# Another order of the partitions between a 64-point and a 47-point DFT, in a kernel of a Fourier layer and an MLP

## The chip, the cores and the metric

The kernel runs on one core of one Trainium2 chip, as one program with one launch. The metric is the device time of one execution in microseconds; a time given for a kernel is the median of several runs. Beside the times there is one profiled execution, from which the spans, the busy times and the waits come.

## The reference

The input is `x`, 8 batches of 3008 tokens with 256 features, in float32. A Fourier layer works along the tokens, and a two-layer MLP follows on every token:

```
X  = rfft(x, axis=1)
Yr = Xr @ w_r - Xi @ w_i + b_r
Yi = Xr @ w_i + Xi @ w_r + b_i
Y  = soft threshold of Yr and of Yi by 0.01
y  = irfft(Y, n=3008, axis=1)
h  = y @ w_in            # 256 -> 2048
out = (h * cos(h)) @ w_out   # 2048 -> 256
```

## The kernel before

**The transform.** 3008 is 64 x 47, and 64 and 47 have no common factor, so the DFT of length 3008 is a DFT-64 and a DFT-47 over a two-dimensional index (n1, n2), with no twiddle factors in between. The host sorts the tokens of `x` by this index (n2 padded from 47 to 48) and, at the end, sorts the output back. Every matmul operand is split into a high and a low part in fp32r; a product is three matmuls, high x high, high x low and low x high.

A batch goes through three stages, and between them through two scratch arrays in device memory, `scr1` and `scr2`:

- **Stage A** (`stage_a`, lines 257 to 295) is the DFT-64. A chunk `c`, of 12, loads 128 partitions x 512 (`xt`, L266; the partitions are two groups g of 64 values n1, the 512 are two values of n2 and 256 features), splits it (`prep`, L268 to 275: a cast to `xh` on VectorE, the residue `xl` on VectorE or GpSimd), multiplies with the constant `f1` (L289 to 291), copies the result out of PSUM to `ao` (L293) and stores it to `scr1` (L294, 256 KB). The output partitions are a real or imaginary part, a group g and a frequency s of 32: 2 x 2 x 32 = 128. In `f1` they are in the order (part, group, s).
- **Stage B** (`stage_b`, lines 298 to 483) is the DFT-47, the complex weights, the threshold and the inverse DFT-47. It loads two frequencies s at a time from `scr1`, as 96 partitions (part, n2) x 2 x 256 (`at`, L306, 192 KB, 16 of a batch), and stores 16 pieces of 192 KB (`bo`, L449) to `scr2`, which is [4 (part, group), 24 (n2), 32 (s), 256].
- **Stage C** (`stage_c`, lines 488 to 531) is the inverse DFT-64. It loads one of the 24 values of n2 at a time from `scr2`, as 128 partitions (part, group, s) x 256 (`bt`, L497, 128 KB; two loads fill one `bt` tile, four make a block of 512 tokens), casts and splits them (`bh`, L503; `bl`), multiplies with the constant `ei` (L521, L522) and leaves `xTh` and `xTl`, 512 tokens with the features on the partitions, for the MLP.

The **MLP** (`moe_step` and `second`, lines 537 to 580) takes the six token blocks of a batch one after the other, with 16 steps of 128 hidden features each.

**The order of the work.** Stages are Python generators that yield an estimated cost after each piece. The prologue runs `stage_a(0)`, then `stage_b(0)` with `stage_a(1)` woven in and with part of the preparation of the MLP's weights (`raw`, L172), then `stage_c(0, 0)`. From there the MLP steps lead: each pulls pieces from `ahead(b)` (lines 615 to 637) as a budget allows. `ahead(b)` yields stage C of the batch's next token blocks, stage B of batch b + 1 and stage A of batch b + 2, and at the end, after a gap, stage C of the first block of batch b + 1. The moment at which the MLP goes from batch b to b + 1 is called a batch turn here; there are seven. Around a turn the loads for two token blocks, eight `bt` loads, follow each other on the queue.

All loads and stores of the stages and the MLP's output stores are issued by SyncE (SP), in one queue; the constants and the tables `f2` are issued by GpSimd. The `TileContext` is built with `schedule_with_timeline_sim=True` (L692): a planner with modelled durations writes the order on each engine. The prologue's tiles come from one pool of five buffers (`XP_BUFS`), which `xt`, `ao`, the Fourier weights and stage B's `at` and `bo` of batch 0 share in turn; later batches use four buffers for loads (`xt`, `at` and `bt` together) and three for results.

How a store or a load walks its two sides is set by these lines:

```
        dst = scr1[b].rearrange("s (r i) d -> r s i d", r=4)                    # L259
            ... dma_start(dst[:, :, 2 * c:2 * c + 2, :], ao ...)                # L294
                nc.sync.dma_start(ld[hf][:, j], scr2[b][:, 4 * t + 2 * hf + j]) # L497
```

The device memory side of the stage A store thus has 4 (part, group) outermost, then 32 s, then a run of 512 numbers; that of the stage C load has 4 outermost, then 32 rows of 256 numbers that follow each other in memory.

Of the kernel before, what the change touches and what calls it, by code (L numbers as in the profile page):

```python
# [19 lines left out]
NB, N, D, FF = 8, 3008, 256, 2048  # L20
# [29 lines left out]
def _split(a):  # L50
    hi = _r11(a)
    return hi, _r11(a - hi.astype(np.float64))
# [7 lines left out]
def _constants():  # L60
    n1, s = np.arange(64), np.arange(32)
    ang = 2 * np.pi * (np.outer(n1, s) % 64) / 64
    f1 = np.zeros((2, 64, 2, 2, 32))
    ei = np.zeros((2, 2, 32, 2, 64))
    alt = (-1.0) ** n1
    for g in range(2):
        f1[g, :, 0, g, :] = np.cos(ang)
        f1[g, :, 1, g, :] = -np.sin(ang)
        f1[g, :, 1, g, 0] = alt
        ei[0, g, :, g, :] = np.cos(ang).T  # L70
        ei[1, g, :, g, :] = -np.sin(ang).T
        ei[1, g, 0, g, :] = alt
    f1 = f1.reshape(128, 128)
    ei = ei.reshape(128, 128) * (2.0 / N)
    crt = {(k % 64, k % 47): k for k in range(N)}
    th = 2 * np.pi * (np.outer(np.arange(47), np.arange(47)) % 47) / 47
    C, S = np.cos(th), np.sin(th)
    f2 = np.zeros((32, 2, 48, 2, 48))
    sig = np.ones((32, 48))
    for sl in range(1, 32):  # L80
        for k2 in range(47):
            sig[sl, k2] = 1 if crt[sl, k2] <= N // 2 else -1
        f2[sl, 0, :47, 0, :47] = C
        f2[sl, 1, :47, 0, :47] = S
        f2[sl, 0, :47, 1, :47] = -S * sig[sl, :47]
        f2[sl, 1, :47, 1, :47] = C * sig[sl, :47]
    i1 = np.zeros((2, 2, 48, 2, 48))
    i1[1, 0, :47, 0, :47] = C
    i1[1, 0, :47, 1, :47] = S
    i1[1, 1, :47, 0, :47] = -S  # L90
    i1[1, 1, :47, 1, :47] = C
    for r, k1 in ((0, 0), (1, 32)):
        for j in range(24):
            c = r * 24 + j
            sig[0, c] = 1 if crt[k1, j] <= N // 2 else -1
            f2[0, r, :47, 0, c] = C[:, j]
            f2[0, r, :47, 1, c] = -S[:, j] * sig[0, c]
            i1[0, 0, c, r, :47] = (0.5 if j == 0 else 1.0) * C[j]
            if j:
                i1[0, 1, c, r, :47] = -S[j]  # L100
    f2 = np.concatenate([f2, f2[:, :, :, :1] + f2[:, :, :, 1:]], 3)
    f2 = f2.reshape(32, 96, 144).transpose(1, 0, 2)
    i1 = i1.reshape(2, 96, 96).transpose(1, 0, 2)
    c_f1 = np.stack(_split(f1), 1)
    c_f3 = np.concatenate(_split(f2), 2)
    c_f2 = np.concatenate(_split(f2[:, :, :96]), 2)
    c_i1 = np.stack(_split(i1), 1)
    c_ei = np.concatenate(_split(ei), 1)
    c_sig = np.concatenate([np.ones((48, 32)), sig.T]).astype(np.float32)
    return [np.ascontiguousarray(a) for a in (c_f1, c_f2, c_i1, c_ei, c_sig, c_f3)]  # L110
# [3 lines left out]
def tile_body(ctx: ExitStack, tc, x, w_r, w_i, b_r, b_i, w_in, w_out,  # L114
              c_f1, c_f2, c_i1, c_ei, c_sig, c_f3, out):
    nc = tc.nc
# [9 lines left out]
    f1 = cp.tile([128, 2, 128], F32R, name="f1")  # L126
# [4 lines left out]
    ei = cp.tile([128, 256], F32R, name="ei")  # L131
# [76 lines left out]
    def rest_pool(lo, x, hi):  # L208
        return nc.gpsimd.tensor_tensor(out=lo, in0=x, in1=hi.bitcast(F32), op=ALU.subtract)  # L209
# [4 lines left out]
    scr1, scr2 = {}, {}  # L214
# [3 lines left out]
    def fps(name):  # L218
        if "pro" in pool:
            if not banks:  # L220
                banks.extend(("f", "h", "o0", "f", "h", "o1", "f", "h"))
            tag = banks.pop(0)
            return ps.tile([128, 512], F32, tag=tag, name=name, bufs=1 if tag[0] == "o" else 3)
        return ps.tile([128, 512], F32, tag="f", name=name, bufs=3)

    def stage_in(name, b=0):
        if b == 0:
            return pool["pro"].tile([128, 512], F32, tag="xp", name=name, bufs=XP_BUFS)
        return wk.tile([128, 512], F32, tag="xt", name=name, bufs=4)

    def stage_out(name, b):
        if b == 0:
            return pool["pro"].tile([128, 512], F32, tag="xp", name=name, bufs=XP_BUFS)
        return wk.tile([128, 512], F32, tag="ao", name=name, bufs=3)
# [19 lines left out]
    mark = {}  # L254


    def stage_a(b):
        scr1[b] = dr.tile([32, 96, 256], F32, tag="scr1", name=f"scr1_{b}")
        dst = scr1[b].rearrange("s (r i) d -> r s i d", r=4)  # L259
        ld = {}  # L260

        def load(c):
            if c < 12:
                ld[c] = stage_in("xt", b)
                with tc.issue_after(mark["at"].ins) if b == 1 and c < 4 else ExitStack():
                    nc.sync.dma_start(ld[c], x[b, :, 512 * c:512 * (c + 1)])  # L266

        def prep(c):  # L268
            if c < 12:
                xt = ld.pop(c)  # L270
                xh = wk.tile([128, 512], F32R, tag="xh", name="xh", bufs=3)
                xl = wk.tile([128, 512], F32R, tag="xl", name="xl", bufs=3)
                nc.vector.tensor_copy(xh, xt)  # L273
                mark[b, c] = (rest if b < 2 and c not in POOL_REST else rest_pool)(xl, xt, xh)
                ld[c] = (xh, xl)

        ahead = XP_BUFS if b == 0 else 1
        for c in range(ahead):
            load(c)
        if b:  # L280
            yield 0.0
        prep(0)
        yield 1.0
        for c in range(12):
            load(c + ahead)
            prep(c + 1)
            xh, xl = ld.pop(c)
            p = fps("pa")
            mm(p, f1[:, 0], xh, start=True, stop=False)  # L289
            mm(p, f1[:, 1], xh, start=False, stop=False)  # L290
            mm(p, f1[:, 0], xl, start=False, stop=True)
            ao = stage_out("ao", b)
            nc.scalar.copy(ao, p)  # L293
            mark[b, "out"] = nc.sync.dma_start(dst[:, :, 2 * c:2 * c + 2, :], ao.rearrange("p (i d) -> p i d", i=2))  # L294
            yield 0.65


# [190 lines left out]
    def stage_c(b, t):  # L488
        th = pool["mo"].tile([128, 2, 512], F32R, tag="xTh", name="xTh", bufs=2)
        tl = pool["mo"].tile([128, 2, 512], F32R, tag="xTl", name="xTl", bufs=2)  # L490
        xT[b, t] = (th, tl)
        ld = {}

        def load(hf):
            ld[hf] = wk.tile([128, 2, 256], F32, tag="xt", name="bt", bufs=4)
            for j in range(2):
                nc.sync.dma_start(ld[hf][:, j], scr2[b][:, 4 * t + 2 * hf + j])  # L497

        def prep(hf):
            bt = ld.pop(hf)  # L500
            bh = wk.tile([128, 2, 256], F32R, tag="xh", name="bh", bufs=3)
            bl = wk.tile([128, 2, 256], F32R, tag="xl", name="bl", bufs=3)
            nc.vector.tensor_copy(bh, bt)  # L503
            rest_pool(bl, bt, bh)
            ld[hf] = (bh, bl)

        load(0)
        load(1)
        yield 2.5
        prep(0)  # L510
        yield 1.0
        for hf in range(2):
            if hf == 0:
                prep(1)
            bh, bl = ld.pop(hf)
            for j in range(2):
                p = fps("pc")
                pv = p.rearrange("p (c h n) -> p c h n", c=2, h=2)
                for c in range(2):
                    cs = slice(128 * c, 128 * c + 128)  # L520
                    mm(p[:, 256 * c:256 * c + 256], bh[:, j, cs], ei, start=c == 0, stop=False, skip_group_check=True)  # L521
                    mm(p[:, 256 * c:256 * c + 128], bl[:, j, cs], ei[:, :128], start=False, stop=c == 1,  # L522
                       skip_group_check=True)
                o = (2 * hf + j) * 128
                hv, lv = pv[:, :, 0], pv[:, :, 1]
                thv, tlv = th[:, :, o:o + 128], tl[:, :, o:o + 128]
                nc.scalar.copy(thv, hv)
                tt = wk.tile([128, 2, 128], F32, tag="tc", name="tc", bufs=2)
                nc.vector.tensor_tensor(out=tt, in0=hv, in1=thv.bitcast(F32), op=ALU.subtract)
                nc.vector.tensor_tensor(out=tlv, in0=lv, in1=tt, op=ALU.add)  # L530
                yield 0.43
# [114 lines left out]
    for b in range(NB):  # L646
        fa = ahead(b)
        for t in range(NTT):
# [20 lines left out]
            while open_[0]:  # L669
                c = next(fa, None)  # L670
# [30 lines left out]
```

## Time and profile before

| | |
|---|---|
| median of 3 runs | 2876.61 us (2874.47 to 2876.82) |
| the profiled execution, time | 2875.72 us |
| the profiled execution, span | 2873.8 us |
| TensorE (PE) busy | 2753.5 us, 96% |
| VectorE (DVE) busy | 2108.0 us, 73% |
| ScalarE (ACT) busy | 1798.6 us, 63% |
| GpSimd (POOL) busy | 1216.5 us, 42% |
| mean granted TensorE clock | 0.972 |
| bytes moved by DMA | 182.42 MB, 63 GB/s over the span |
| stage A stores (`scr<-ao`) | 96 of 256 KB |
| stage C loads (`bt<-scr`) | 192 of 128 KB |

How to read the profile: the span goes from the first to the last instruction of the profiled execution, and times in the trace count from its start. "Busy" is the time in which an engine has an instruction in work; the ends of matmuls are modelled. The granted clock is the share of full speed that the throttle left TensorE. PEld is TensorE's weight load, SPq the queue of DMA issues of SyncE. A line of the waits names the waiting engine, its tile and line, then what released it, and the total in us, the number of waits and the longest. A line of the chain of waits has a start, a duration and what the end of the program hung on in that time; for a DMA it is the time from issue to landing. A line of the timeline has a start, a duration, the engine, the line of the kernel, the operation, output and input, a count and, in brackets, how long the engine idled before it and what released it. A line of the windows has the stretch, its length, busy time and number of instructions of each engine in it, and then the granted clock, the mean busy share of the core's 16 DMA engines, and GB/s.

### The profile page before, as it was taken

How to read it: one execution, taken by the hardware profiler on the slowest of the kernel's cores; microseconds unless marked ns; L12 is line 12 of the kernel's file. 1: busy time of each engine (PE TensorE's matmuls, PEld its weight loads, DVE VectorE, ACT ScalarE, POOL GpSimd, SP SyncE). 2: the span in 40 equal slices, each digit the busy share in tenths (PEclk: the TensorE clock that was granted, in tenths of full speed). 3: DMA queues.
4: the chain of work that ended last, by engine and by line, in shares of the span. 5: the costliest groups of instructions: out<-in, count | busy, mean ns of one | idle time of the engine just before them, and what ended most of it. 6: DMA issues, size and time to landing. Idle time of an engine off the chain costs nothing.

```text
span 2873.8 us, 39659 instructions
## 1 busy us (share of the span) xinstructions
PE 2753.5 (96%) x13439; PEld 2346.1 (82%) x13439; DVE 2108.0 (73%) x3816; ACT 1798.6 (63%) x3526; POOL 1216.5 (42%) x1031
## 2 busy tenths in 40 slices
PE   4759999999999999999999999999999999999999
PEld 2647888888888888888888888888888888888888
DVE  3769777677876877678776778768787677766665
ACT  2547666566666666566665666666666666666666
POOL 2635554245433554254442445434543354322222
PEclk6869999999999999999999999999999999999999
DMA  5541122212212122112221122221221211010000
GB/s 163 161 129 59 54 74 80 63 49 75 72 48 69 57 75 76 48 54 62 82 63 58 42 71 71 60 65 49 75 72 48 69 50 52 30 52 26 8 15 14
DMA packets 118921, 182.42 MB, mean 63 GB/s; under 512 B 10336, under 2 KB 62400, under 8 KB 118720
## 3 DMA queue, kind: packets, MB, share of 16 engines
q1 hardware_dynamic: 111152, 159.43, 18.2%
q0 software_dynamic: 7568, 20.47, 2.8%
q8 instruction: 106, 1.74, 0.2%
q14 instruction: 95, 0.78, 0.1%
HBM read 104.89 MB, written 74.97 MB: 63 GB/s over the span
## 4 chain that ended last, share of the span: by engine, by line
PE 87%; DMA 6%; DVE 3%; ACT 1%; SPq 1%; issue 1%; POOL 1%; ACTq 0%; DVEq 0%; POOLq 0%
PE ph L562 11%; PE ph L564 11%; PE ph L563 11%; PE po L544 11%; PE po L548 11%; PE po L545 11%; PE pi L444 3%; DMA bt<-scr 2%; PE pw L393 2%; PE pw L391 2%; PE pw L392 2%; PE pb L356 2%; PE pt L426 2%; PE pc L521 2%; DMA scr<-ao 2%
## 5 line engine op out<-in xcount | busy, mean ns | idle before, releaser
L209 POOL TENSOR_TENSOR gl<-u,gh 128x512 fp32r<-128x512 f32 (+1 forms) x384 | 493.5, 1285 | 885.1 <-ACT gh L574 627.2
L570 DVE SCALAR_TENSOR_TENSOR u<-ph,u 128x512 f32<-128x512 f32 (+1 forms) x768 | 518.4, 675 | 252.1 <-ACT u L569 247.9
L573 DVE TENSOR_TENSOR u<-ph,u 128x512 f32<-128x512 f32 (+1 forms) x768 | 519.0, 676 | 221.5 <-ACT u L572 209.2
L572 ACT ACTIVATE u<-u 128x512 f32<-128x512 f32 (+1 forms) x768 | 479.7, 625 | 311.7 <-DVE u L570 308.2
L569 ACT ACTIVATE u<-ph 128x512 int32<-128x512 f32 (+1 forms) x768 | 451.3, 588 | 268.5 <-PE ph L564 247.8
L562 PE MATMUL ph<-xTh,win 128*128 128x512 f32 (+1 forms) x1536 | 601.9, 393 | 6.5 <-DVE u L573 5.6
L563 PE MATMUL ph<-xTl,win 128*128 128x512 f32 (+1 forms) x1536 | 599.3, 390 | 2.4 <-DVE xTl L530 2.4
L574 ACT CAST gh<-u 128x512 fp32r<-128x512 f32 (+1 forms) x768 | 468.1, 610 | 212.4 <-DVE u L573 205.2
L564 PE MATMUL ph<-xTh,win 128*128 128x512 f32 (+1 forms) x1536 | 600.7, 391 | 0.0
L544 PE MATMUL po<-gh,wout 128*128 128x512 f32 (+1 forms) x1536 | 599.7, 390 | 0.0
L545 PE MATMUL po<-gh,wout 128*128 128x512 f32 (+1 forms) x1536 | 599.0, 390 | 0.0
L548 PE MATMUL po<-gl,wout 128*128 128x512 f32 (+1 forms) x1536 | 485.8, 391 | 0.3 <-DVE gl L212 0.3
L212 DVE TENSOR_TENSOR gl<-u,gh 128x512 fp32r<-128x512 f32 (+1 forms) x384 | 317.9, 828 | 31.8 <-ACT gh L574 25.5
L562 PEld LDWEIGHTS ph<-xTh,win 128*128 128x128 f32 x1536 | 289.9, 189 | 58.9 <-DVE u L573 8.4
L544 PEld LDWEIGHTS po<-gh,wout 128*128 128x128 f32 x1536 | 290.5, 189 | 53.6 <-ACT gh L574 0.3
L563 PEld LDWEIGHTS ph<-xTl,win 128*128 128x128 f32 x1536 | 290.2, 189 | 53.3 <-DVE xTl L530 3.0
L564 PEld LDWEIGHTS ph<-xTh,win 128*128 128x128 f32 x1536 | 290.4, 189 | 52.9
L545 PEld LDWEIGHTS po<-gh,wout 128*128 128x128 f32 x1536 | 290.3, 189 | 51.1
L548 PEld LDWEIGHTS po<-gl,wout 128*128 128x128 f32 x1536 | 286.2, 189 | 51.6 <-DVE gl L212 0.9
L209 POOL TENSOR_TENSOR al<-at,ah 96x512 fp32r<-96x512 f32 x128 | 168.1, 1314 | 204.4 <-PE pb L358 62.8
L209 POOL TENSOR_TENSOR bl<-bt,bh 128x512 fp32r<-128x512 f32 x96 | 127.7, 1330 | 274.8 <-DVE bh L503 173.4
L209 POOL TENSOR_TENSOR xl<-xt,xh 128x512 fp32r<-128x512 f32 x82 | 106.8, 1306 | 99.9 <-DVE xh L273 31.8
(101 smaller groups left out, 3772.7 us busy)
## 6 DMA issues: line engine op xcount, KB each, us to landing
xt<-in_dram SPq DMA_DIRECT2D x96, 256.0 KB
scr<-ao SPq DMA_DIRECT2D x96, 256.0 KB
at<-scr SPq DMA_DIRECT2D x128, 192.0 KB
scr<-bo SPq DMA_DIRECT2D x128, 192.0 KB
bt<-scr SPq DMA_DIRECT2D x192, 128.0 KB
out_dram<-ob SPq DMA_DIRECT2D x80, 256.0 KB
f<-in_dram POOLq DMA_DIRECT2D x56, 288.0 KB, 3.7
raw<-in_dram SPq DMA_DIRECT2D x16, 512.0 KB
```

The costliest lines, as they stand in the source:

```text
L209: return nc.gpsimd.tensor_tensor(out=lo, in0=x, in1=hi.bitcast(F32), op=ALU.subtract)
L544: mm(po[e][:, :n], wout[:, 0, f, es], gh[:, :n], start=f == 0, stop=False)
L545: mm(po[e][:, :n], wout[:, 1, f, es], gh[:, :n], start=False, stop=False)
L548: mm(po[e][:, :n], wout[:, 0, f, es], gl[:, :n], start=False, stop=f == NFC - 1)
L562: mm(h, win[:, 0, c, fs], th[:, c, :n], start=c == 0, stop=False)
L563: mm(h, win[:, 0, c, fs], tl[:, c, :n], start=False, stop=False)
L564: mm(h, win[:, 1, c, fs], th[:, c, :n], start=False, stop=c == 1)
L569: nc.scalar.activation(k[:, :n], h, AF.Identity, bias=0.25, scale=1.0 / TWO_PI)
L570: nc.vector.scalar_tensor_tensor(out=u[:, :n], in0=h, scalar=1.0 / TWO_PI, in1=k[:, :n], op0=ALU.mult, op1=ALU.subtract)
L572: nc.scalar.activation(u[:, :n], u[:, :n], AF.Sin, bias=HALF_PI, scale=TWO_PI)
L573: nc.vector.tensor_tensor(out=u[:, :n], in0=h, in1=u[:, :n], op=ALU.mult)
L574: nc.scalar.copy(gh[:, :n], u[:, :n])
```

## The change

The 128 partitions between the DFT-64 and the DFT-47 go from the order (part, group, s) to (s, part, group), on both sides of stage B. The constant `f1` has its output columns and `ei` its rows put in that order, on the host. The stage A store then walks `scr1` with s and (part, group) as one outermost run of 128 rows; the stage C load walks `scr2` with 32 s outermost and 4 rows (part, group), 24 x 32 x 256 numbers apart, inside. The layouts of `scr1` and `scr2`, stage B, and the number and size of all instructions and DMAs are unchanged.

```diff
-    f1 = f1.reshape(128, 128)
-    ei = ei.reshape(128, 128) * (2.0 / N)
+
+    f1 = f1.reshape(128, 4, 32).transpose(0, 2, 1).reshape(128, 128)
+    ei = ei.reshape(4, 32, 128).transpose(1, 0, 2).reshape(128, 128) * (2.0 / N)
...
     def stage_a(b):
         scr1[b] = dr.tile([32, 96, 256], F32, tag="scr1", name=f"scr1_{b}")
-        dst = scr1[b].rearrange("s (r i) d -> r s i d", r=4)
+        dst = scr1[b].rearrange("s (r i) d -> (s r) i d", r=4)
...
-            mark[b, "out"] = nc.sync.dma_start(dst[:, :, 2 * c:2 * c + 2, :], ao.rearrange("p (i d) -> p i d", i=2))
+            mark[b, "out"] = nc.sync.dma_start(dst[:, 2 * c:2 * c + 2, :], ao.rearrange("p (i d) -> p i d", i=2))
...
-                nc.sync.dma_start(ld[hf][:, j], scr2[b][:, 4 * t + 2 * hf + j])
+                nc.sync.dma_start(ld[hf][:, j], scr2[b][:, 4 * t + 2 * hf + j].rearrange("r s d -> s r d"))
```

## The prediction

> **What bounds the kernel now.** I read the busy slices first, then the waits of TensorE, then the chain of waits at the places that these name, and last the DMA share in short windows there.
>
> ```profile
> span 2873.8 us, 39659 instructions
> ...
> PE   4759999999999999999999999999999999999999
> ...
> PEclk6869999999999999999999999999999999999999
> ```
> ```profile
> PE pc L521 <- DVE bh L503: 35.8, 9, 17.6
> PE pb L346 <- ACT ah L313: 23.8, 2, 23.5
> ```
>
> Each digit covers 71.8 us. TensorE has room only in the first three slices, and there its granted clock is low too; from the fourth on it is full to the digit. Its two longest waits are for `bh` (35.8 us in 9 waits, one of 17.6), the first cast of a stage C load, and for `ah` (one of 23.5), the first cast of the prologue's stage B. Both casts stand behind a DMA of the kind that the change touches: `ah` needs all stage A stores of the batch, `bh` needs a stage C load. The chain of waits in the prologue:
>
> ```profile
> 10.86 6.51 DMA scr<-ao
> 18.08 6.75 DMA scr<-ao
> 25.41 0.60 ACT ao L293
> 26.12 8.76 DMA scr<-ao
> 35.59 14.27 DMA scr<-ao
> 50.57 7.60 DMA scr<-ao
> 59.33 4.00 DMA at<-scr
> ```
>
> From 10.86 to 58.17 the chain is five landings of stage A stores, 43.89 of 47.3 us: a new `ao` or `xt` tile waits for the old store to leave its buffer, and at the end stage B's first load waits for the last store. What the DMA engines do meanwhile:
>
> ```profile
> 40.00:42.00 2.00, 0.00 (x0) 0.00 (x0) 0.00 (x0) 0.00 (x0) 0.00 (x0) 0.50 0.26 101
> 44.00:46.00 2.00, 0.00 (x0) 0.00 (x0) 0.00 (x0) 0.00 (x0) 0.00 (x0) 0.50 0.73 263
> 60.00:70.00 10.00, 7.90 (x36) 7.70 (x36) 2.58 (x6) 4.91 (x10) 8.19 (x7) 0.50 0.69 200
> 550.00:552.00 2.00, 0.09 (x1) 0.12 (x2) 0.66 (x2) 0.00 (x0) 0.15 (x1) 1.00 0.27 97
> 570.00:867.00 297.00, 297.00 (x1475) 252.43 (x1474) 231.00 (x423) 196.34 (x386) 136.78 (x116) 1.00 0.21 61
> ```
>
> The last two columns are the mean busy share of the 16 engines and GB/s. At 40 us only stage A stores are in flight, at 550 us mostly stage C loads, and everything waits for them; yet the share is 0.26 and 0.27 (4.2 and 4.3 engines of 16) at 101 and 97 GB/s. With other transfers beside them (44 to 46 us) the same engines reach 0.73 and 263 GB/s. So these transfers sit on about four engines, at some 25 GB/s each, and a 256 KB store needs 2.6 us of them. Between two batch turns (570 to 867) TensorE is busy without a gap at clock 1.00: there is nothing to win there, and whatever is saved elsewhere is saved from the end.
>
> **The change, part by part.** Instructions, their sizes and bytes are the same; `f1` and `ei` only have their columns and rows in another order, made on the host. What changes is the outermost run of the store's target (4 rows before, 128 after) and of the load's source (4 before, 32 after). The Trainium skill, "DMA: Bandwidth & Descriptors", section "Why a DMA increments its semaphore by 16 and not by 1", says that a DMA uses the largest number of engines, up to 16, that divides the slowest dimension of both sides: 4 before and 16 after here. The shares of 0.26 and 0.27 agree for before; by that rule a 256 KB store would need 0.65 us of its engines.
>
> *Prologue stage A.* No row shows these two transfers on more engines, so I bound a landing by the nearest rows with 96 rows outermost: below by `bo` (192 KB), which is issued at 540.56 and whose landing lets SyncE issue at 542.83, 2.27 us; above by the first `at` load of a burst, 4.00 us (above).
>
> ```profile
> 540.56 0.30 SPq L449 DMA_DIRECT2D scr<-bo  x1
> 541.30 0.53 SPq L294 DMA_DIRECT2D scr<-ao  x1
> 542.83 10.10 SPq L497 DMA_DIRECT2D bt<-scr  x8
> ```
> ```profile
> 98.76 6.87 DMA xt<-in_dram
> 111.60 3.11 DMA scr<-bo
> ```
> ```profile
> 8.45 0.43 PE pa L291
> ```
> ```profile
> L209 POOL TENSOR_TENSOR xl<-xt,xh 128x512 fp32r<-128x512 f32 x82 | 106.8, 1306 | 99.9 <-DVE xh L273 31.8
> ```
>
> I take 3.2, near the 3.11 of a `bo` store in the busy prologue. Five landings then cost 16 instead of 43.9 us, and the stores alone would end at 30.3. But something else is late next. Matmuls: 12 chunks of 3 at 0.43 us are 15.5 us, no bound. The five buffers of the prologue pool: each chunk holds one for a load (about 5 us between 3.11 and the 6.87 of a contended `xt`, and about 1.8 for the cast and the 1.31 of the residue) and one for the result (1.1: a copy of 0.60 and an issue of 0.53; then 3.2 for the landing), 11.1 us over 5 buffers or 2.2 per chunk. The first chunk's three matmuls begin at about 7.6 (the one shown is the third); 12 chunks end at 34, and the last store lands at 37. Lower bound 32 (2.27 per landing, loads of 4: 9.2/5 or 1.8 per chunk); upper 45 (6.87 and 4.00: 13.8/5 or 2.8 per chunk). So stage B's first load leaves at 37 instead of 58.2: 21 us saved, between 13 and 26.
>
> *Prologue stage B (to 178).* Batch 1's stage A stores share four engines with everything that also needs those four; without that backlog `xt` loads like the 6.87 one should land sooner. But most of this stretch waits for engines, so I take 3 us, from -2 (the raw weights, which land while stage B starts, hold up ScalarE) to 10.
>
> *From stage B to the first stage C.*
>
> ```profile
> 180.80 9.45 DMA scr<-bo
> ```
> ```profile
> 196.29 0.80 PE L521 MATMUL pc<-ei,bh 128*128 128x256 f32 x2 [17.62 <-DVE bh L503]
> 199.18 0.55 PE L521 MATMUL pc<-ei,bh 128*128 128x256 f32 x1 [2.09 <-DVE bh L503]
> ```
>
> The last `bo` store takes 9.45 us where another took 3.11, behind the `ao` backlog; the first matmul on a stage C load comes 6.0 us after it lands, and a second gap of 2.09 follows. With 3.2 for the store (6.2 saved), 3.9 from landing to matmul (two issues of 0.3, a landing of 2.9 inside the bounds above, a cast; 2.1 saved) and the later pairs close behind (3.7 saved: the 2.09 and part of the wait for the third and fourth pair), I take 12, between 7 and 15.
>
> *The seven batch turns.* SyncE needs 10.10 us to issue 8 stage C loads (128 KB each), since the queue is full, and what stands behind it, four `at` loads, waits too. 1 MB at 97 GB/s is 10.8 us, behind the 2.6 us of the `ao` store issued at 541.30.
>
> ```profile
> 551.34 0.43 DVE L503 CAST bh<-bt 128x512 fp32r<-128x512 f32 x1 [6.25 <-DMA bt<-scr]
> ```
> ```profile
> 549.10 0.37 PE L545 MATMUL po<-gh,wout 128*128 128x448 f32 x1
> 551.91 0.36 PE L521 MATMUL pc<-ei,bh 128*128 128x256 f32 x1 [2.45 <-DVE bh L503]
> ```
> ```profile
> 540.00:570.00 30.00, 24.02 (x109) 20.45 (x107) 16.03 (x32) 12.00 (x26) 9.96 (x8) 0.89 0.35 108
> 867.00:897.00 30.00, 26.93 (x131) 24.19 (x130) 16.92 (x33) 14.12 (x30) 11.01 (x9) 0.94 0.27 83
> 1208.00:1238.00 30.00, 27.07 (x133) 24.33 (x132) 17.08 (x33) 14.48 (x30) 11.03 (x9) 0.94 0.27 84
> 1549.00:1579.00 30.00, 27.07 (x127) 24.57 (x127) 16.29 (x32) 13.80 (x29) 10.59 (x9) 0.89 0.28 84
> 1891.00:1921.00 30.00, 27.14 (x133) 24.44 (x132) 17.23 (x34) 14.49 (x31) 11.03 (x9) 0.94 0.27 84
> 2232.00:2262.00 30.00, 27.14 (x128) 24.69 (x127) 17.32 (x34) 14.42 (x31) 11.00 (x9) 0.89 0.27 84
> 2552.00:2582.00 30.00, 27.73 (x134) 24.85 (x133) 18.05 (x36) 17.09 (x35) 12.64 (x10) 0.94 0.29 102
> sum 210.00, PE 187.10 PEld 167.52 DVE 118.91 ACT 100.42 POOL 77.25; mean PE 26.73 PEld 23.93 DVE 16.99 ACT 14.35 POOL 11.04
> ```
>
> In these 210 us TensorE idles 22.9, and each stall is followed by a low clock: 30 x (3 x 0.11 + 4 x 0.06) = 17.1 us of full-clock work. Together 40 (little overlaps). TensorE runs dry at 549.10 + 0.2, some 6.3 us after SyncE begins to issue the loads. After the change a first pair needs two issues (0.3 to 0.53 each), a landing of 2.3 to 4.0 and a cast of 0.43: 3.3 to 5.5 us. That is inside 6.3, so the stall goes with its clock step; the other six turns lose less than this first one, so I take it for all. Next late are the other casts and GpSimd's residues; I leave 1 us a turn for them: 33 saved, between 20 and 40.
>
> *Sum.* 21 + 3 + 12 + 33 = 69 of the span of 2873.8, so 2804.8; the profiled execution took 2875.72, 1.9 more than its span and 0.9 under the median. In terms of the median: 2876.6 - 69, about 2807.
>
> **Rivals.** *Scattered reads (stage C gains nothing).* The load now takes rows of 1 KB from four places 786 KB apart in turn, where a run of 32 KB was contiguous. If that made it as slow as four engines did, only stage A, stage B and the last `bo` store gain: 21 + 3 + 6 = 30, 2847. Against it: `at` loads also take 1 KB rows, 98 KB apart, and 60 to 70 us shows 200 GB/s with them.
>
> *Slower: scattered reads so slow that stage C is late beyond what stage A wins.* Place: the seven turns. The 30 us won are used up from the point at which the first cast comes 30/7 = 4.3 us later per turn than now, 12.8 us after the first issue instead of 8.5. If the loads took twice as long (half of 97 GB/s), each turn would lose 8.5 more: 2847 + 60 = 2907. Against it, the same row: 16 engines would have to do worse than four do now.
>
> *It does nothing.* The same page of the Trainium skill, section "Rules for kernel authors", says that transfers to partition halves both spray over all 16 engines; read alone, the 128-partition sides of these two would already do that, and 2877 would stay. The mechanism: the number of engines follows the SBUF side, and the four busy engines are another limit, such as writes to one place. Against it: the load and the store, whose only likeness is the 4 outermost, both stop at 0.26 to 0.27, and `at` and `xt` don't.
>
> **How the numbers follow.** About 0.2% (6 us) is what a measurement can tell from no change. Forecast 0.85 (2807); scattered reads 0.08 (2847); nothing 0.04 (2877); slower 0.03 (2907). Best case: 26 + 10 + 15 + 40 = 91, 2786; worst within the forecast: 13 - 2 + 7 + 20 = 38, 2839. The range reaches over the first rival too: 2786 to 2850. Faster 0.93, same 0.04, slower 0.03.
>
> **What would show it.** Right: the chain's `scr<-ao` landings fall to 3 or 4 us and stage B's first load leaves near 37; the last `bo` store lands in about 3; eight `bt` issues take under 5 us; clock digits of 9 at all seven turns with no wait of `pc` for `bh` over 1 us. Wrong: a share near 0.27 while a stage A store or a stage C load is alone in flight; the prologue still near 58 with short landings, which would mean buffers or loads; or a turn that keeps its stall with early loads, which would mean that the order on VectorE, not the DMA, sets it. All of this takes the order of the instructions on each engine as it is; a planner writes it, and another order would move every term.

## The result and the profile after

The changed kernel takes 2797.16 us in the median of 4 runs (2793.97 to 2798.55), the kernel before 2876.72 (2874.47 to 2877.56, 4 runs): a ratio of 0.9723, 95% interval 0.9706 to 0.974, or 79.6 us less. A second set of runs of the changed kernel gave 2797.06 beside 2876.28, 0.9724 (0.971 to 0.9737). The profiled execution took 2798.55 us with a span of 2796.8, so the span is 77.0 shorter.

The page of the changed kernel, the same lines as before:

```profile
span 2796.8 us, 39657 instructions
...
PE   6879999999999999999999999999999999999999
...
PEclk7789999999999999999999999999999999999999
```

The first three slices are fuller. The granted clock is higher in the first and the third slice and lower in the second; the slices are 69.9 us long now, 71.8 before. The instructions are the same work; line numbers from 73 on are one higher than before (L498 is the load that was L497).

The chain of waits over the prologue's stage A, in the changed kernel, shows what took the place of the five landings of stores:

```profile
1.66 6.16 DMA xt<-in_dram
...
9.03 3.58 DMA xt<-in_dram
13.07 2.94 DMA xt<-in_dram
...
17.99 3.66 DMA xt<-in_dram
...
25.80 7.71 DMA scr<-ao
33.61 0.59 ACT ao L294
34.22 2.08 DMA scr<-ao
36.90 0.44 SPq L307
37.43 4.46 DMA at<-scr
```

Two store landings are left in the chain where there were five, 9.79 us where there were 43.89. The last store of all takes 2.08 us; the other still takes 7.71. Loads of `xt` make up 16.3 of the chain's first 22 us. Stage B's first load leaves at 36.51 (the queue of SyncE, the first `at` loads, before and after):

```profile
58.39 1.83 SPq L306 DMA_DIRECT2D at<-scr  x4
```
```profile
36.51 2.31 SPq L307 DMA_DIRECT2D at<-scr  x5
```

The seven batch turns of the changed kernel, at the places to which they have moved, 30 us each (two of the seven rows, and the sum):

```profile
500.00:530.00 30.00, 27.96 (x147) 24.38 (x146) 22.45 (x44) 18.16 (x39) 13.66 (x11) 1.00 0.36 110
818.00:848.00 30.00, 30.00 (x159) 27.68 (x158) 21.66 (x40) 19.68 (x40) 12.21 (x10) 1.00 0.35 108
...
sum 210.00, PE 207.96 PEld 191.01 DVE 153.39 ACT 131.51 POOL 94.42; mean PE 29.71 PEld 27.29 DVE 21.91 ACT 18.79 POOL 13.49
```

The sum of TensorE was 187.10. The whole idle time that is left, 2.04 us, lies in the first turn; the other six have 30.00 of 30.00, and the clock is 1.00 at all seven. SyncE's queue at the first turn and VectorE's first cast of it:

```profile
503.72 0.34 SPq L295 DMA_DIRECT2D scr<-ao  x1
505.28 5.05 SPq L498 DMA_DIRECT2D bt<-scr  x8
510.44 1.84 SPq L307 DMA_DIRECT2D at<-scr  x2
```
```profile
508.46 0.43 DVE L504 CAST bh<-bt 128x512 fp32r<-128x512 f32 x1 [0.95 <-DMA bt<-scr]
```

The eight loads are issued in 5.05 us instead of 10.10, the store's issue takes 0.34 instead of 0.53, and the first cast comes 3.2 us after the first issue instead of 8.5. VectorE still waits 0.95 us for it, but TensorE has no wait for `bh` there: its 2.04 us are three other waits of at most 1.1 us, and no low clock follows them.

Where the 77.0 us went can be read from landmarks. Stage B's first load leaves 21.9 earlier. Stage B's last matmul ends the prologue's stretch. Here is its line on TensorE before, and after together with the first matmul on a stage C load, which stood at 196.29 before:

```profile
178.13 0.54 PE L444 MATMUL pi<-yl,i 96*96 96x512 f32 x1
```
```profile
154.62 0.44 PE L445 MATMUL pi<-yl,i 96*96 96x512 f32 x1
162.68 0.58 PE L522 MATMUL pc<-ei,bh 128*128 128x256 f32 x1 [7.62 <-DVE bh L504]
```

Stage B's last matmul comes 23.5 earlier, so stage B itself gave 1.6. The loads of the first turn leave at 505.28 instead of 542.83, 37.5 earlier: the passage to stage C and the first MLP steps gave 14.0. The end comes 77.0 earlier, so the seven turns gave 39.5. The profile of the second set of runs gives 20.9, 4.1, 14.2 and 39.5 for the same four places, so the gains of stage A and stage B are known only to within 1 and 2.5 us.

### The profile page after: what moved, and what is told of

Same layout as the page of the kernel before. It is cut to its first block, busy times and chain, and to the rows that moved or that the text cites. A ratio compares the mean times of both kernels' runs of the same rounds, so it can differ in the third digit from the quotient of the medians.

```text
span 2796.8 us, 39657 instructions
## 1 busy us (share of the span) xinstructions
PE 2736.2 (98%) x13439; PEld 2336.3 (84%) x13439; DVE 2115.5 (76%) x3816; ACT 1800.1 (64%) x3526; POOL 1223.0 (44%) x1031
## 4 chain that ended last, share of the span: by engine, by line
PE 92%; DVE 3%; DMA 3%; issue 1%; ACT 1%; POOL 0%; SPq 0%; ACTq 0%; DVEq 0%; POOLq 0%
PE ph L563 12%; PE po L549 12%; PE po L545 12%; PE po L546 12%; PE ph L564 12%; PE ph L565 12%; PE pi L445 3%; PE pw L392 2%; PE pw L394 2%; PE pw L393 2%; PE pb L357 2%; PE pc L522 2%; PE pt L427 2%; PE pb L359 1%; DMA xt<-in_dram 1%
```

## The experiments

The theory: the outermost count of the two sides sets the number of DMA engines, at some 25 GB/s each, and three places wait for those transfers: the end of stage A, the passage to the first stage C, and the turns. The rivals: the scattered reads, the planner's new order, and the full queue of SyncE as a cost of its own.

**Each half of the change alone.** The store with `f1`, and the load with `ei`, are independent, since the scratch arrays keep their layouts. The store alone, as a diff against the changed kernel:

```diff
-    ei = ei.reshape(4, 32, 128).transpose(1, 0, 2).reshape(128, 128) * (2.0 / N)
+    ei = ei.reshape(128, 128) * (2.0 / N)
...
-                nc.sync.dma_start(ld[hf][:, j], scr2[b][:, 4 * t + 2 * hf + j].rearrange("r s d -> s r d"))
+                nc.sync.dma_start(ld[hf][:, j], scr2[b][:, 4 * t + 2 * hf + j])
```

> Stage A's store and f1 as in the changed kernel, stage C's load and ei as before: 128 rows outermost for the stores, 4 for the loads. Theory (each transfer runs on as many engines as its outermost count allows, and its landing is what the three places wait for): stage B's first load leaves near 36.5 us as in the changed kernel, the last bo store of the prologue lands in about 3 us instead of 9.45; eight bt loads still need about 10 us to issue and the share at a turn stays near 0.27, but they no longer stand behind 2.6 us of an ao store, so a turn loses 4 to 5 us instead of 5.6. Time about 2840 (2825 to 2850). Rival (the gain of the prologue comes from the planner's new order, which follows from both edits together): stage B's first load stays near 58 us, or the time is not the sum of parts: above 2855.

Measured: 2827.35 us (ratio 0.9834, 0.982 to 0.9849), 48.6 less than the kernel before beside it. SyncE's queue and the windows at the first turn:

```profile
36.50 5.84 SPq L307 DMA_DIRECT2D at<-scr  x6
...
507.67 6.89 SPq L498 DMA_DIRECT2D bt<-scr  x8
```
```profile
511.00:513.00 2.00, 2.00 (x12) 1.85 (x11) 0.00 (x0) 0.55 (x1) 0.00 (x0) 1.00 0.26 93
```

Stage A is as fast as in the changed kernel (36.50 against 36.51), the loads while alone still keep 0.26 of the engines busy, and the last `bo` store lands in 2.38 us. The turns gave more than expected: the span is 50.7 shorter, of which 35.2 by the first turn's loads (542.83 to 507.67), so 15.5 in seven turns, where 4 to 11 were expected. Taking away the 2.6 us of the store ahead of the loads is worth 2.2 us a turn on average, and the turns keep 24 of their 39.5 us.

The load alone, against the changed kernel:

```diff
-    f1 = f1.reshape(128, 4, 32).transpose(0, 2, 1).reshape(128, 128)
+    f1 = f1.reshape(128, 128)
...
-        dst = scr1[b].rearrange("s (r i) d -> (s r) i d", r=4)
+        dst = scr1[b].rearrange("s (r i) d -> r s i d", r=4)
```

> Stage C's load and ei as in the changed kernel, stage A's store and f1 as before: 32 rows outermost for the loads, 4 for the stores. Theory: stage B's first load stays at 58 us, the last bo store still takes about 9 us; the eight bt loads issue in about 5 us and the turns lose almost nothing, though the loads stand behind an ao store on four engines. Time about 2836 (2828 to 2848); the gains of this kernel and of the one with the store alone add up to the whole gain of 79.6 us within 8. Rival (a turn's stall comes from the ao store ahead of the loads, not from the loads' own four engines): the turns keep more than half of their 39.5 us, time above 2855.

Measured: 2839.12 us (0.987, 0.9855 to 0.9884), 36.9 less. Stage B's first load leaves at 57.23, so stage A kept its 58 us; the last `bo` store takes 6.89 us, less than the 9 that were expected.

```profile
531.90 0.53 SPq L295 DMA_DIRECT2D scr<-ao  x1
533.45 6.09 SPq L498 DMA_DIRECT2D bt<-scr  x8
```

Behind a store that still sits on four engines the turns keep 6.6 of their 39.5 us, about one a turn, and the low clock is gone. TensorE's wait for the casts after 240 us:

```profile
PE pc L522 <- DVE bh L504: 0.9, 2, 0.7
```

(The profiled execution of this kernel was its fastest, 2833.63 us.) The two gains add up to 85.5 us against 79.6, within the 8 that were expected. By the spans of the profiles the excess is 15.9 us: 8.8 of it at the turns (15.5 + 32.8 against 39.5) and 7.1 before them (35.2 + 9.4 against 37.5). At a turn it can be explained: the store ahead of the loads and the loads' own four engines are two parts of one lateness, and either one taken away brings back a part that the other would bring too. That the same holds for the passage to the first stage C, which also has stores ahead of loads, was not shown.

**The planner's order.** The traces show it. Up to stage B's first load, every engine works off the same instructions (by line, operation and tile) in the same order before and after the change, but for one stage A store that stands later in SyncE's queue. From the first turn's loads to the end the order is the same on every engine. It differs only in between, in the rest of the prologue and the first MLP steps, and it came with the store's edit: the store alone has the order of the changed kernel throughout, the load alone that of the kernel before. So the order has no part in the gain of the turns, next to none in that of stage A, and can touch only the 15.6 us of stage B and the passage.

**Two rows outermost for the load instead of 32.** The changed kernel's `f1` and store stay; `ei` is as before.

```diff
-    i1 = i1.reshape(2, 96, 96).transpose(1, 0, 2)
+    i1 = i1.reshape(2, 2, 48, 2, 2, 24).transpose(0, 1, 2, 3, 5, 4).reshape(2, 96, 96).transpose(1, 0, 2)
...
-        scr2[b] = dr.tile([4, 24, 32, 256], F32, tag="scr2", name=f"scr2_{b}")
-        dst = scr2[b].rearrange("r i s d -> (r i) s d")
+        scr2[b] = dr.tile([2, 24, 64, 256], F32, tag="scr2", name=f"scr2_{b}")
+        dst = scr2[b].rearrange("r i (g s) d -> (r i g) s d", g=2)
...
-                nc.sync.dma_start(ld[hf][:, j], scr2[b][:, 4 * t + 2 * hf + j].rearrange("r s d -> s r d"))
+                nc.sync.dma_start(ld[hf][:, j], scr2[b][:, 4 * t + 2 * hf + j])
```

> As the changed kernel, but with stage B's output rows in the order (part, n2, group) and scr2 laid out as (part, n2, group, s), so that the load has 2 rows outermost and 64 rows of 1 KB that follow each other inside; same bytes, same number of DMAs. Theory: a load runs on two engines: share near 0.13 and about 48 GB/s while the loads are alone, eight loads take 21 us instead of 10.8, and the turns lose 10 to 15 us each: time about 2910 (2870 to 2940), slower than with the store alone by 40 or more. Rival (reads that follow each other in memory are what counts, or the SBUF side sets the engines): as the changed kernel or the store alone, 2797 to 2850.

Measured: 2923.01 us (1.0168, 1.0151 to 1.0185), 126 slower than the changed kernel and 96 slower than the store alone. Every engine has the order of instructions of those two kernels, so 4, 32 and now 2 rows outermost in the load are compared with little else changed (the layout of `scr2` and the order within the constants). The windows and SyncE's queue at the first turn:

```profile
528.00:530.00 2.00, 0.73 (x4) 0.34 (x2) 0.00 (x0) 0.00 (x0) 0.00 (x0) 1.00 0.14 48
```
```profile
522.12 16.42 SPq L498 DMA_DIRECT2D bt<-scr  x8
```

0.14 of 16 is 2.2 engines, at 48 GB/s. From the first turn's loads to the end this kernel takes 105 us longer than the changed one, about 15 a turn, the upper end of what was expected. The 64 rows that follow each other in memory helped nothing. This is the strongest support for the theory: with 2, 4 and 32 rows outermost the loads moved at 48, 97 and 203 GB/s (the last beside other transfers; a window of the changed kernel, with a share of 0.70, or 11 engines):

```profile
508.00:510.00 2.00, 2.00 (x12) 1.85 (x11) 1.13 (x3) 1.22 (x3) 1.62 (x2) 1.00 0.70 203
```

**Rows that follow each other, with 128 rows outermost.** Again `ei` is as before.

```diff
-    i1 = i1.reshape(2, 96, 96).transpose(1, 0, 2)
+    i1 = i1.reshape(2, 2, 48, 4, 24).transpose(0, 1, 2, 4, 3).reshape(2, 96, 96).transpose(1, 0, 2)
...
-        scr2[b] = dr.tile([4, 24, 32, 256], F32, tag="scr2", name=f"scr2_{b}")
-        dst = scr2[b].rearrange("r i s d -> (r i) s d")
+        scr2[b] = dr.tile([24, 4, 32, 256], F32, tag="scr2", name=f"scr2_{b}")
+        dst = scr2[b].rearrange("i r s d -> (i r) s d")
...
-                nc.sync.dma_start(ld[hf][:, j], scr2[b][:, 4 * t + 2 * hf + j].rearrange("r s d -> s r d"))
+                nc.sync.dma_start(ld[hf][:, j], scr2[b][4 * t + 2 * hf + j].rearrange("r s d -> (r s) d"))
```

> As the changed kernel, but the 128 rows of a stage C load follow each other in memory: stage B's output rows in the order (n2, part, group), scr2 laid out as (n2, part, group, s), ei as before. Theory (number of engines counts, scattered 1 KB rows cost nothing that shows): the load runs on 16 engines as well, time within 6 us of the changed kernel, 2791 to 2803. Rival (scattered rows cost): the bt landings fall clearly below the median of 2.6 us and the kernel is faster by 8 us or more.

Measured: 2800.58 us (0.974, 0.9726 to 0.9755), the changed kernel's time within 4 us and not faster. The DMA issues of the changed kernel and of this one, the last number being the median from issue to landing:

```profile
bt<-scr SPq DMA_DIRECT2D x192, 128.0 KB, 2.6
```
```profile
bt<-scr SPq DMA_DIRECT2D x192, 128.0 KB, 2.2
```

With rows that follow each other a load lands 0.4 us sooner, and nothing of that reaches the end. (The planner wrote another order for this kernel, so the two times differ by more than the rows.)

**Is a turn's loss lateness alone?** The first try, on the kernel before, moved the generator's steps so that the loads should leave earlier against the casts.

```diff
-GAP = 5
+GAP = 2
...
-        yield 2.5
+        yield 2.5 if t else 5.5
```

> The kernel before with all transfers on four engines, but at a batch turn the stage C loads leave earlier against the work that needs them: GAP 2 instead of 5 and a first yield of 5.5 instead of 2.5 in the first block of a batch, so that everything from the casts on stays where it was and only the loads move 3 units ahead (some 5 us). Theory (a turn loses time only because the loads come 3 to 5 us too late, stall and clock step together): the turns lose nearly nothing, the prologue is as before: time about 2842 (2834 to 2852). Rival (slow loads also cost by holding up SyncE's queue, and with it at loads and stores): less than half of 39.5 us comes back, above 2857.

Measured: 2875.19 us (0.9997, 0.9988 to 1.0006): nothing. The loads left at 539.23 and the first cast came 8.5 us after, with the same 6.26 us of waiting. On every engine the instructions stand in the same order as in the kernel before: what the planner wrote did not change. So this run tested neither theory nor rival. The second try held the casts back instead, tying them on VectorE to the latest `u` of the MLP:

```diff
-GAP = 5
+GAP = 2
...
-            nc.vector.tensor_copy(bh, bt)
+            with tc.issue_after(mark["u"].ins) if b and t == 0 else ExitStack(): nc.vector.tensor_copy(bh, bt)
...
-        yield 2.5
+        yield 2.5 if t else 10.5
...
-        nc.vector.tensor_tensor(out=u[:, :n], in0=h, in1=u[:, :n], op=ALU.mult)
+        mark["u"] = nc.vector.tensor_tensor(out=u[:, :n], in0=h, in1=u[:, :n], op=ALU.mult)
```

> The kernel before with all transfers on four engines; in the first block of a batch the casts of the stage C loads are held back on VectorE behind the latest product u of the MLP, and the first yield is 10.5 instead of 2.5 with GAP 2 instead of 5. VectorE then meets the first cast of a turn five u products (some 12 us) later, while the loads leave where they did. Theory (a turn's 5.6 us are lateness only: the loads land 8.5 to 17 us after their issue, and the casts stand too early for that): the waits of pc for bh at the turns fall under 0.5 us and the clock stays at 1.00; time about 2842 (2835 to 2856). Rival (four busy engines and a SyncE queue held for 10 us cost by themselves, whatever the casts do): less than half of 39.5 us comes back, above 2857.

Measured: 2841.17 us (0.9884, 0.9869 to 0.9899), 34.4 less, with the stage A stores and the stage C loads still on four engines. Its first two turns, and SyncE's queue and the held casts at the second:

```profile
540.00:570.00 30.00, 24.18 (x110) 20.68 (x109) 16.70 (x32) 11.91 (x26) 9.95 (x8) 0.89 0.35 108
860.00:890.00 30.00, 30.00 (x153) 27.47 (x152) 20.16 (x35) 20.09 (x42) 11.14 (x9) 1.00 0.31 98
```
```profile
868.67 8.88 SPq L497 DMA_DIRECT2D bt<-scr  x8
```
```profile
881.22 2.18 DVE L503 CAST bh<-bt 128x512 fp32r<-128x512 f32 x3
```

The first turn was not moved by the edit, against the expectation (its first cast still waits 6.28 us), and lost what it lost before; it serves as a control inside the run. At the second, the loads leave where they left before (868.87), the first cast comes 12.6 us after them instead of 8.5, SyncE is held for 8.88 us, and TensorE is full at clock 1.00. So it stays: from 575 to 2820 us, over six turns, TensorE is busy for 2245.00 of 2245.00 us at clock 1.00. At these six turns the loss was lateness of the loads against the casts and nothing else; busy DMA engines and a held SyncE cost nothing there.

**What ends stage A now?** Two edits of the changed kernel.

```diff
-                ld[c] = stage_in("xt", b)
+                ld[c] = stage_in("xt", b or c % 2)
...
-            ao = stage_out("ao", b)
+            ao = stage_out("ao", b or c % 2)
```

> As the changed kernel, but every other xt and ao tile of the prologue's stage A comes from the pools of the later batches: 5 + 4 + 3 buffers instead of 5. Theory of the prediction (the five buffers are what is late next in stage A): ScalarE's waits of ao for a store (6.66 us the longest) go, the first at load leaves at 31 to 34 instead of 36.5; time 2790 to 2796. Rival (from 25 to 33 us the DMA engines are full, 302 to 358 GB/s, with the f2 tables and the weights beside the last stores): the first at load stays within 1 us of 36.5 and the time at 2797.

Measured: 2798.26 us (0.9732, 0.9715 to 0.9748), no gain. Both theory and rival were half right. Windows, then SyncE's queue at the first `at` loads and at the last `bo` store:

```profile
29.00:31.00 2.00, 0.00 (x0) 0.00 (x0) 0.40 (x1) 0.00 (x0) 0.00 (x0) 0.50 0.94 362
```
```profile
32.59 2.31 SPq L307 DMA_DIRECT2D at<-scr  x5
...
153.52 0.35 SPq L173 DMA_DIRECT2D raw<-in_dram  x1
153.96 0.38 SPq L450 DMA_DIRECT2D scr<-bo  x1
158.24 5.11 SPq L498 DMA_DIRECT2D bt<-scr  x8
```

The buffers were worth 3.9 us of stage A (32.59 instead of 36.51), and after them the engines are full, at 318 to 362 GB/s from 25 to 31 us; the last `ao` store, issued at 24.84, takes 7.6 us there. But the stage C loads left at 158.24, where they left at 158.21: the 3.9 us were given back by the end of stage B. Stage B's last matmul begins at 152.48 instead of 154.62, so 2.1 of them were left there; then a load of raw weights stands ahead of the last `bo` store in this order, and that store takes 4.13 us.

The second edit loads the Fourier weights and the constants later:

```diff
-W_LOAD_AT = 10
+W_LOAD_AT = 12
```

> As the changed kernel, with W_LOAD_AT 12 instead of 10: the Fourier weights and the constants i1 and ei are loaded after the last chunk of stage A instead of before the last two. Theory (full DMA engines hold up the last stores): the store that lands in 7.71 us lands in 3 to 5, the first at load leaves at 32 to 35; time 2791 to 2797, unless the later weights hold up wmix. Rival (buffers alone, or the f2 tables alone): the first at load stays near 36.5.

Measured: 2805.19 us (0.9758, 0.9743 to 0.9773), 8 slower than the changed kernel. The first `at` load leaves later, not earlier, at 37.99, and only two leave before 42 us:

```profile
37.99 0.86 SPq L307 DMA_DIRECT2D at<-scr  x2
```

ScalarE's waits of `ao` for a store fell from 14.3 to 7.7 us, and the last store is issued at 26.89 instead of 34.22, so the weights did stand in the stores' way. It then takes 7.0 us, since the engines are as full as before (336 to 383 GB/s from 27 to 35 us), but it has landed before 34. What keeps the `at` loads until 37.99 is something else: a load of raw weights ahead of them in SyncE's queue, for which SyncE waits 6.3 us until VectorE has made `wa` from the load before it (`raw` has one buffer).

**More buffers, with the raw weights behind the last store.** The same edit as for more buffers, and one more:

```diff
-EARLY_STEPS = 80
+EARLY_STEPS = 77
```

> As the kernel with more buffers in stage A, with EARLY_STEPS 77 instead of 80, by which the last early load of raw weights stands behind the last bo store of the prologue on SyncE's queue instead of ahead of it. Theory (the 4 us that more buffers won in stage A were given back because the last bo store landed in 4.13 us behind a 512 KB load, and all stage C loads wait for it): that store lands in 2 to 3 us, the first matmul on a stage C load comes 2 us or more earlier than in the changed kernel (162.68), time 2790 to 2796, faster than the changed kernel by 2 to 5 us. Rival (the place where stage B ends is set elsewhere, by VectorE and ScalarE): 2797 as before.

> The changed kernel once more, beside the one with more buffers, to compare the two on one chip: 2797 (2793 to 2801).

Measured side by side: 2798.17 us (0.9727, 0.9713 to 0.974) with the edits, 2797.06 us (0.9724, 0.971 to 0.9737) for the changed kernel. The theory fell: `at` loads leave at 32.24 (37.51 in the changed kernel beside it), but the stage C loads at 156.70 (156.77), and nothing is left in the time. TensorE's waits between 30 and 240 us show one place where it went:

```profile
PE pi L445 <- ACT yh L434: 6.0, 4, 3.4
```

In the first profile of the changed kernel that wait totals 0.2 us. Also, the two profiled executions of the changed kernel differ at the first matmul on a stage C load by 1.4 us (162.68 and 161.31), so a gain of this size can't be read from one profile. What in stage B gives back the 4 to 5 us (the weights' preparation on ScalarE and VectorE, or the planner's order) stays open.

## Why the prediction was right, point by point

The sum forecast 69 us; the span is 77.0 shorter and the median 79.6 lower. The mechanism held, and most of what was missing lies in one term, the turns.

- **Stage A: 21 forecast (13 to 26), 21.9 measured.** The end of 37 was right (the first `at` load left at 36.51). The working behind it was right in part: five buffers were late next, but for 3.9 us, where the prediction's working put 6.7 on them (37 against 30.3). The rest is the full DMA engines: the prediction had not counted the tables and weights that load in the same microseconds. The landing taken as 3.2 us was too long for an uncrowded store (2.08 for the last) and too short for a crowded one (7.71). That the end came within 1 us is in part luck.
- **Stage B: 3 forecast (-2 to 10), 1.6 measured.** With an earlier start it passes on at most 2.1 of the 3.9 us won ahead of it. That engines bound it fits this, but was not shown.
- **Passage to stage C: 12 forecast (7 to 15), 14.0 measured.** The first matmul on a stage C load came 10.1 us earlier against the end of stage B, where 8.3 were forecast: the last `bo` stores land in 2.1 to 2.4 us (9.45 before, 3.2 forecast). The later pairs gave the remaining 3.9, where 3.7 were forecast.
- **Turns: 33 forecast (20 to 40), 39.5 measured.** This is the term that was mis-sized: 1 us a turn was left for the casts and residues that would be late next, and nothing was late next at six turns. Idle time and lost clock together, 22.9 + 17.1 = 40, were the right size without a deduction: 20.9 of the idle time and all of the clock came back, 38.0 of the 39.5 us. (The row of 549.10 with the wait of 2.45 puts the moment at which TensorE runs dry at 549.46, 6.6 us after the first issue and not 6.3; that changes nothing.) That the stall and the clock step belong to one lateness is shown by the held casts: they brought back 34.4 us, and the first turn, which they left alone, kept its loss.
- **Rival, scattered reads:** excluded; rows that follow each other gave 2800.58 us with 128 rows outermost. The slower version of it needed loads slower than on four engines; they moved at about twice that rate, beside other transfers.
- **Rival, nothing happens:** excluded. The rule of the Trainium skill, "DMA: Bandwidth & Descriptors", that was drawn on (section "Why a DMA increments its semaphore by 16 and not by 1") agrees with the shares of 0.14 with 2 rows outermost and 0.26 to 0.27 with 4. The sentence on partition halves in its section "Rules for kernel authors" can't be read the way this rival read it: a side of 128 partitions did not put these transfers on all engines when the other side had 4 rows outermost. That the changed transfers use all 16 was not read from a window of their own; 0.70 of 16 beside other transfers is the nearest row.
- **The planner's order** did change in the prologue, after stage B's first load. It isn't the cause of the gains of stage A and of the turns, where the order is the old one. How much of the 1.6 us of stage B and the 14.0 us of the passage comes from it was not separated.
- **The signs named:** stage B's first load near 37, the last `bo` store in about 3 us (2.1 to 2.4), clock 1.00 at all seven turns and no wait of `pc` for `bh` over 1 us came as said. Eight `bt` issues took 5.05 us, just over the 5, and one store landing of 7.71 us stayed in the chain where 3 or 4 were expected. That SyncE's queue was "full" is an inference from the length of its issues; no row shows the queue itself.

## What to carry to other kernels

Look at the DMA share while one transfer is alone in flight: 0.26 of 16 engines meant four of them here, and the fix was the order of an index; the sizes of the transfers stayed as they were. Then ask who waits for a landing: here three places did, all at the borders of stages, and in the steady stretch the slow transfers cost nothing. At a border a wait of 2.3 to 3 us cost nearly twice that, because the clock stepped down behind it (0.94 or 0.89 in the mean of 30 us), while the short waits left in the changed kernel (1.1 us at most) had no such step; and what comes back can be had on the consumer's side too, by placing the consumer later.

## What the runs showed of the hardware that was not expected

By these windows an engine of the sixteen moved an estimated 24 GB/s: 48 with two rows outermost, 93 to 101 with four. Few rows outermost lengthen the issues too. Behind the changed store, eight loads of 128 KB took SyncE 16.42 us with 2 rows outermost, 6.89 with 4 and 5.05 with 32; the 10.10 us of the kernel before had the old store on four engines ahead of them as well. Even the issue of the store ahead of them fell from 0.53 us (the kernel before and the load alone) to 0.34 (the changed kernel, the store alone and the run with 2 rows).
